# Delta-rule attention with an MLP: products with the state by head, in row and column tiles of 64

## The chip, the cores and the metric

The kernel runs on one core of a Trainium2 chip. The metric is the device time of one execution in microseconds; for the kernel before it is the median of nine executions. A profile is one execution taken by the hardware profiler. In it PE is the matmul side of TensorE and PEld its weight loads, DVE is VectorE, ACT is ScalarE, POOL is GpSimd and SP the engine that issues most DMAs.

## The reference

Four sequences (b), eight heads (h), 768 steps, head size 48. Each head has a state matrix of 48x48 that a delta rule updates step by step; its outputs, laid side by side to 384 columns, go through an MLP with a quick GELU.

```python
k_n = k / (np.linalg.norm(k, axis=-1, keepdims=True) + 1e-06)
state = np.zeros((B, H, D, D))
for t in range(S):
    y[:, :, t] = np.einsum('bhd,bhde->bhe', q[:, :, t], state)
    v_old = np.einsum('bhde,bhd->bhe', state, kt)          # kt, vt, bt: step t of k_n, v, beta
    state = state + bt * np.einsum('bhd,bhe->bhde', kt, vt - v_old)
x = y.transpose(0, 2, 1, 3).reshape(B * S, H * D)          # 3072 x 384
h = x @ w_in                                               # 384 x 2048
out = (h * (1.0 / (1.0 + np.exp(-1.702 * h)))) @ w_out     # 2048 x 384
```

## The kernel before

**Units.** The steps are cut into six chunks of 128. A unit is one chunk c of one sequence b, 24 units in all, c in the outer loop and b in the inner one. Within a chunk the recurrence is written as a triangular system: with G the products of keys by keys and keys by queries, and V the values, one solves for U, the corrected values times beta. The chunk has four blocks of 32 steps. The 32x32 diagonal blocks are inverted on VectorE for two sequences at a time (`invert`); the inverses go out to DRAM and come back as XB.

**One unit.** `prepare` transposes keys and queries to kqT (two heads to a partition half each: the head h lies on the partitions from h % 2 * 64, in the slot h // 2) and forms G in psG (L368). The class `Step` does the rest.

- `keys` (L501): V must lose the product of the keys with the state of the chunks before. S_bd keeps the state of two heads as a block-diagonal matrix of 128 rows by 2 x 48 columns, so four matmuls of the full array with 96 columns give all heads. They go to a bank psR that the unit keeps for its whole life.
- `above` (L512) adds to psR, block by block, the products with the U of the blocks above; `rest` (L520) takes 32 rows of psR from V on VectorE; `solve` (L524) multiplies by the inverse, in 32x32 tiles, and `solved` (L531) copies U on ScalarE.
- `queries` (L537): the transposed product of the state with the queries, per head, 48 output rows on the partition half of the head, into one bank psY; `outputs` adds U by G to the same places, then copies psY to xT, the input of the MLP.
- `state` (L556): four matmuls of the full array give keys by U for two heads each; VectorE adds the two diagonal blocks to S_bd (L564), in two instructions.

An xT tile has 128 partitions and three slots of 384/128. Six of the eight heads go to rows 0 to 47 and 64 to 111 of the three slots; the last two are copied to `last` (L576), and six DMAs bring their rows in pieces of 16 into the rows 48 to 63 and 112 to 127 of xT (L583). The rows of w_in are loaded in the order that fits (`x_rows`).

**The MLP.** `hidden` (L599) is xT by w_in into ph, followed by the GELU on ScalarE; `written` (L614) is its result by w_out into po. Both are generators, cut in small pieces. The weights come as float64 and are made float32 by VectorE and ScalarE (`from_double`); this lasts into the fifth slot or so.

**Order.** `slot(n)` interleaves the stages of three units that overlap: A is unit n-1, B_ is unit n, D_ is unit n+1. It has six groups, after each of which some matmuls of the MLP are taken from a queue (`take`), and pieces of the inversion, of the norms and of the weight conversion are put in. Group 0 is `above` and `rest` of block 2 of A; group 1 `solve` of block 2 of A beside `above` of block 1 of B_; group 2 `above` of block 3 of A, then `keys` and `rest(0)` of D_, then the last psG pair of `prepare`; group 3 three `solve`s in three tiles of the array and `queries` of A; group 4 `state` of A; group 5 `outputs` of A. The first two slots are pinned to this order. After that a planner orders each engine's instructions by its own costs, with the order of the program as priority, and gives out the PSUM banks: `ps_seq` has four, for psR, psU, psY and psS, `ps_big` two for psT and psG, `ps_moe` two.

Of the kernel before, what the change touches and what calls it, by code (L numbers as in the profile page):

```python
# [18 lines left out]
def kernel(  # L19
# [122 lines left out]
    S_bd = cpool.tile([128, B, NP, 2, D], F32, name="S_bd")  # L142
# [21 lines left out]
    def from_double(dst, raw, n, alone):  # L164
# [38 lines left out]
        (hh * DP + o, r, m, step)  # L203
        for hh in range(2)
        for o, r, m, step in (
            (0, hh * D, D, 2 * D), (D, (2 * KC + hh) * D, XR, XR),
        )
# [280 lines left out]
    class Step:  # L488


        def __init__(self, n, xT):
            self.c, self.b = units[n]
            self.xT = xT
            self.kn, self.kqT, self.G = ready.pop(n)
            self.V, self.XB = loaded.pop(n), inverse.pop(n)
            self.psR = bank("psR")
            self.U = wk.tile([128, H, D], F32, tag="U", name="U", bufs=3)

        def with_state(self, ps, i):
            for j in range(NP):  # L500
                pe.matmul(  # L501
                    ps[:, 2 * j : 2 * j + 2, :], lhsT=self.kqT[:, j, i, :],
                    rhs=S_bd[:, self.b, j], start=(j == 0), stop=True, skip_group_check=True,
                )

        def keys(self):
            if self.c > 0:
                self.with_state(self.psR, 0)

        def above(self, blk, h):  # L510
            r, a = slice(blk * BS, (blk + 1) * BS), slice(0, blk * BS)
            pe.matmul(  # L512
                self.psR[r, h, :], lhsT=self.G[a, h, 0, r], rhs=self.U[a, h, :],
                start=(self.c == 0 and h == 0), stop=True, skip_group_check=True,
            )

        def rest(self, blk):
            r = slice(blk * BS, (blk + 1) * BS)
            if self.c > 0 or blk > 0:
                vec.tensor_tensor(self.V[r], self.V[r], self.psR[r], op=ALU.subtract)  # L520
# [12 lines left out]
        def turned(self, lhsT, rhs, start):  # L533

            for h in range(H):
                j, p = h // 2, h % 2 * 64
                pe.matmul(  # L537
                    self.psY[p : p + D, j, :], lhsT=lhsT(h), rhs=rhs(h),
                    start=start and j == 0, stop=True, skip_group_check=True,
                )  # L540

        def queries(self):
            self.psY = bank("psY", (128, NP, 128))
            if self.c > 0:
                self.turned(
                    lambda h: S_bd[h % 2 * 64 : h % 2 * 64 + D, self.b, h // 2, h % 2, :],
# [276 lines left out]
```

## Time and profile before

| | |
|---|---|
| median of 9 executions | 858.25 us (854.8 to 860.56) |
| the profiled execution | 860.51 us, span 858.8 us |
| mean granted clock | 0.968 |
| PE busy | 807.4 us, 94% |
| PEld busy | 596.0 us, 69% |
| DVE busy | 495.2 us, 58% |
| ACT busy | 208.6 us, 24% |
| POOL busy | 107.9 us, 13% |
| share of the chain that ended last: PE | 80% |
| po L614, ph L599 | 28% each of the chain |
| psY L537, psR L512, psG L368, psU L524 | 5%, 4%, 4%, 4% of the chain |
| psR L501 (keys), psS L556 | 2% each of the chain |

Busy times are unions: two matmuls that overlap count once, so busy time divided by the count of a group is not the duration of one, and its mean duration has a tail that overlaps the next. The chain is followed back from the last instruction, at each step to what released it. In the timeline the start of one group to the start of the next is what a group takes where PE never idles.

### The profile page before, as it was taken

The numbers are of one execution on the slowest core, as the hardware profiler recorded it, in microseconds if no ns is written. First come the engines' busy times: TensorE is split into PE (matmuls) and PEld (weight loads), VectorE is DVE, ScalarE is ACT, GpSimd is POOL, SyncE is SP. The second block draws the span as 40 slices with busy tenths as digits, with TensorE's granted clock in tenths as the row PEclk, the third lists the DMA queues.
The fourth block names the chain that finished last, engine by engine and source line by source line (L and its number), as shares of the span: only waits on it lengthen the run. The fifth ranks groups of instructions, "written<-read, shape, count | busy, mean of one in ns | idle before, by whom it ended". The sixth has DMA issues, their size and how long they took to land.

```text
span 858.8 us, 15548 instructions
## 1 busy us (share of the span) xinstructions
PE 807.4 (94%) x6564; PEld 596.0 (69%) x6564; DVE 495.2 (58%) x1024; ACT 208.6 (24%) x407; POOL 107.9 (13%) x117
## 2 busy tenths in 40 slices
PE   8309999989999999999999999999999999999998
PEld 7207688557767767767767767767768768677684
DVE  5898789879992782772772872772862850110100
ACT  3202554233312312212213212212212112112020
POOL 2103232130021102101101110111100000000000
PEclk9759789999999999999999999999999999999999
DMA  9897553631323132132132132042032020000000
GB/s 146 180 151 150 145 141 86 150 90 46 70 69 68 31 76 64 27 84 62 20 85 63 20 86 61 19 87 52 11 79 50 2 57 2 10 15 1 22 2 18
DMA packets 160964, 55.75 MB, mean 65 GB/s; under 512 B 128672, under 2 KB 157568, under 8 KB 160896
## 3 DMA queue, kind: packets, MB, share of 16 engines
q1 hardware_dynamic: 154048, 46.02, 26.7%
q0 software_dynamic: 1856, 7.87, 2.9%
q10 hardware_dynamic: 4992, 0.89, 1.0%
q8 instruction: 51, 0.84, 0.4%
q14 instruction: 17, 0.14, 0.1%
HBM read 33.13 MB, written 20.45 MB: 62 GB/s over the span
## 4 chain that ended last, share of the span: by engine, by line
PE 80%; DVE 10%; DMA 7%; issue 2%; POOL 1%; ACT 1%; ACTq 0%; SPq 0%; DVEq 0%; POOLq 0%
PE po L614 28%; PE ph L599 28%; PE psY L537 5%; PE psR L512 4%; PE psG L368 4%; PE psU L524 4%; DMA w_out<-in_moe_w_out_dram 2%; DVE P L104 2%; PE psR L501 2%; PE psT L354 2%; PE psS L556 2%; DVE YB L104 1%; DMA w_out<-in_moe_w_in_dram 1%; DVE w_in L104 1%; DMA bI<-in_beta_dram 1%
## 5 line engine op out<-in xcount | busy, mean ns | idle before, releaser
L614 PE MATMUL po<-w_out,gT 128*128 128x384 f32 x768 | 267.8, 494 | 3.5 <-DVE w_out L192 3.5
L599 PE MATMUL ph<-xT,w_in 128*128 128x256 f32 (+1 forms) x1248 | 270.8, 371 | 0.3 <-DMA xT<-last 0.2
L599 PEld LDWEIGHTS ph<-xT,w_in 128*128 128x128 f32 x1248 | 220.4, 193 | 38.8 <-issue 11.9
L614 PEld LDWEIGHTS po<-w_out,gT 128*128 128x128 f32 x768 | 139.9, 190 | 94.9 <-issue 8.9
L604 ACT ACTIVATE gT<-ph 128x512 f32<-128x512 f32 (+1 forms) x104 | 58.6, 564 | 189.8 <-PE ph L599 189.8
L520 DVE TENSOR_TENSOR V<-V,psR 32x384 f32<-32x384 f32 x88 | 48.4, 550 | 90.6 <-PE psR L512 84.8
L531 ACT COPY U<-psU 32x384 f32<-32x384 f32 x89 | 41.8, 469 | 140.4 <-PE psU L524 88.8
L512 PEld LDWEIGHTS psR<-U,G 64*32 64x32 f32 (+2 forms) x1088 | 49.9, 107 | 21.9 <-issue 19.2
L512 PE MATMUL psR<-U,G 64*32 64x48 f32 (+2 forms) x1088 | 59.7, 205 | 1.5 <-ACT U L531 1.5
L392 POOL TENSOR_SCALAR_AFFINE_SELECT G<-G 128x1024 f32<-128x1024 f32 x24 | 28.0, 1168 | 240.7 <-DVE G L376 128.4
L152 PE MATMUL ps_warm<-ident 128*128 128x256 bf16 x152 | 22.8, 318 | 35.1 <-DVE ps_warm L104 32.8
L368 PE MATMUL psG<-kqT 48*128 48x256 f32 x352 | 54.7, 411 | 0.3 <-DVE G L376 0.3
L621 DVE COPY o<-po 128x384 f32<-128x384 f32 x24 | 13.3, 555 | 70.8 <-PE po L614 70.6
L524 PEld LDWEIGHTS psU<-V,XB 32*32 32x32 f32 x1424 | 34.3, 105 | 22.5 <-issue 10.4
L432 DVE TENSOR_TENSOR P<-NT,YB 64x2 f32<-64x2 f32 (+4 forms) x135 | 46.3, 343 | 4.3
L436 DVE TENSOR_REDUCE YB<-P 64x2 f32<-64x2 f32 (+4 forms) x135 | 43.3, 321 | 4.3
L152 PEld LDWEIGHTS <-ident 128*128 128x128 bf16 x152 | 17.0, 114 | 39.7 <-DVE ps_warm L104 33.2
L524 PE MATMUL psU<-V,XB 32*32 32x48 f32 x1424 | 41.3, 203 | 1.5 <-DVE V L520 1.4
L372 ACT ACTIVATE G<-psG 128x512 f32<-128x512 f32 x44 | 26.3, 597 | 65.3 <-PE psG L368 63.9
L576 DVE COPY last<-psY 48x128 f32<-48x128 f32 x20 | 5.9, 294 | 59.0 <-ACT xT L577 58.1
L368 PEld LDWEIGHTS psG<-kqT 48*128 48x128 f32 x352 | 33.3, 191 | 9.2 <-issue 2.6
L304 POOL TENSOR_TENSOR ksq<-KN 128x384 f32<-128x384 f32 x17 | 14.6, 857 | 177.3 <-DMA KN<-in_k_dram 177.3
(112 smaller groups left out, 784.5 us busy)
## 6 DMA issues: line engine op xcount, KB each, us to landing
Nd<-G SPq DMA_DIRECT2D x24, 512.0 KB, 3.3
w_out<-in_moe_w_out_dram POOLq DMA_DIRECT2D x14, 384.0 KB, 4.5
KN<-in_k_dram SPq DMA_DIRECT2D x24, 192.0 KB, 3.4
V<-in_v_dram SPq DMA_DIRECT2D x24, 192.0 KB, 3.3
out_dram<-o SPq DMA_DIRECT2D x24, 192.0 KB, 1.9
QP<-in_q_dram SPq DMA_DIRECT2D x20, 192.0 KB, 3.1
w_out<-in_moe_w_in_dram SPq DMA_DIRECT2D x6, 576.0 KB, 12.1
NT<-Nd SPq DMA_DIRECT2D x24, 128.0 KB, 2.5
```

Source lines behind the costliest of these rows:

```text
L152: pe.matmul(ps, lhsT=ones[:, 0:128], rhs=ones, start=True, stop=True)
L368: pe.matmul(ps[hh][:, i], lhsT=kqT[pr, g + i, 0, :], rhs=kqT[pr, g + i, :, :], start=True, stop=True,)
L432: tt(P, diag(Nf, i * BS, [[0, i], [1, i]]), diag(Yf, 0, [[BS, i], [1, i]]), op=ALU.mult,)
L436: red(diag(Yf, i, [[BS, i]]), P, axis=AX.X, op=ALU.add, negate=True)
L512: pe.matmul(self.psR[r, h, :], lhsT=self.G[a, h, 0, r], rhs=self.U[a, h, :], start=(self.c == 0 and h == 0), stop=True, skip_group_check=True,
L520: vec.tensor_tensor(self.V[r], self.V[r], self.psR[r], op=ALU.subtract)
L524: pe.matmul(psU[r, h, :], lhsT=self.XB[r, h, :], rhs=self.V[r, h, :], start=True, stop=True,)
L531: act.copy(self.U[r], psU[r])
L537: pe.matmul(self.psY[p : p + D, j, :], lhsT=lhsT(h), rhs=rhs(h), start=start and j == 0, stop=True, skip_group_check=True,)
L599: pe.matmul(ph[:, u], lhsT=w_in[:, j, f * 128 : (f + 1) * 128], rhs=xT[:, j, t], start=(j == 0), stop=(j == KC - 1),)
L604: act.activation(gT[f0 // FQ][:, f0 % FQ : f0 % FQ + 2, t], ph, ACT.Gelu_apprx_sigmoid)
L614: pe.matmul(po, lhsT=gT[f // FQ][:, f % FQ, i * C : (i + 1) * C], rhs=w_out[:, f, :], start=(f == 0), stop=(f == FC - 1),)
```

## The change

The state is kept as ST: head h on its 48 partitions, in the slot h // 2, without the zero blocks, and 16 further columns at the end of each sequence. `keys` has a matmul per head now, with the 48 rows of that head, in two row tiles of the array (0 and 64), each to a bank of its own (psK); their results are subtracted from all 128 rows of V at once, in one instruction for each bank. psR holds only the products of `above` and is taken anew for each block; `rest(0)` is gone. `turned` takes 64 weight columns per head instead of 48 (the last 16 belong to the next head, or to the padding of ST and of the fixed U buffers US), and puts the head h at the column tile h // 4, in the bank h % 2. `queries` goes through its heads in an order that visits all four tiles of 64x64. `state` has a matmul per head in two column tiles, and one addition over 128 partitions. psY is copied 128 partitions wide; the spilled rows are overwritten by the DMAs from `last`. The rows of w_in are permuted to suit.

```diff
-    S_bd = cpool.tile([128, B, NP, 2, D], F32, name="S_bd")
+    ST = cpool.tile([128, B, NP * D + XR], F32, name="ST")
+    US = [cpool.tile([128, H * D + XR], F32, name=f"US{i}") for i in range(3)]
...
     x_rows = [
-        (hh * DP + o, r, m, step)
-        for hh in range(2)
-        for o, r, m, step in (
-            (0, hh * D, D, 2 * D), (D, (2 * KC + hh) * D, XR, XR),
-        )
+        (ct * DP + o, (ct * NP + i) * D, m, step)
+        for ct in range(2)
+        for o, i, m, step in ((0, 0, D, D), (D, KC, XR, XR))
     ]
...
-            self.psR = bank("psR")
-            self.U = wk.tile([128, H, D], F32, tag="U", name="U", bufs=3)
-
-        def with_state(self, ps, i):
-            for j in range(NP):
+            self.US = US[n % len(US)]
+            self.U = self.US[:, 0 : H * D].rearrange("p (h d) -> p h d", h=H)
+
+        def rows(self, h):
+            return slice(h % 2 * 64, h % 2 * 64 + D)
+
+        def keys(self):
+            if self.c == 0:
+                return
+            psK = [bank("psK", (128, NP, D)) for _ in range(2)]
+            for h in range(H):
+                j = h // 2
                 pe.matmul(
-                    ps[:, 2 * j : 2 * j + 2, :], lhsT=self.kqT[:, j, i, :],
-                    rhs=S_bd[:, self.b, j], start=(j == 0), stop=True, skip_group_check=True,
+                    psK[h % 2][:, j, :], lhsT=self.kqT[self.rows(h), j, 0, :],
+                    rhs=ST[self.rows(h), self.b, j * D : (j + 1) * D], start=True, stop=True,
                 )
-        def keys(self):
-            if self.c > 0:
-                self.with_state(self.psR, 0)
-
+            for hh in range(2):
+                Vh = self.V[:, hh::2, :]
+                vec.tensor_tensor(Vh, Vh, psK[hh], op=ALU.subtract)
...
-        def turned(self, lhsT, rhs, start):
-            for h in range(H):
-                j, p = h // 2, h % 2 * 64
+        def turned(self, order, lhsT, rhs, start):
+            for h in order:
+                p, s = h // NP * DP, h % NP // 2
                 pe.matmul(
-                    self.psY[p : p + D, j, :], lhsT=lhsT(h), rhs=rhs(h),
-                    start=start and j == 0, stop=True, skip_group_check=True,
+                    self.psY[h % 2][p : p + DP, s, :], lhsT=lhsT(h), rhs=rhs(h),
+                    start=start and s == 0, stop=True, skip_group_check=True,
                 )
         def queries(self):
-            self.psY = bank("psY", (128, NP, 128))
+            self.psY = [bank("psY", (128, 2, 128)) for _ in range(2)]
             if self.c > 0:
                 self.turned(
-                    lambda h: S_bd[h % 2 * 64 : h % 2 * 64 + D, self.b, h // 2, h % 2, :],
-                    lambda h: self.kqT[h % 2 * 64 : h % 2 * 64 + D, h // 2, 1, :],
+                    (0, 5, 4, 1, 2, 7, 6, 3),
+                    lambda h: ST[self.rows(h), self.b, h // 2 * D : h // 2 * D + DP],
+                    lambda h: self.kqT[self.rows(h), h // 2, 1, :],
                     True,
                 )
         def state(self):
...
-            psS = bank("psS", (128, NP, 2, D))
-            for j in range(NP):
+            psS = bank("psS", (128, NP, D))
+            for h in range(H):
+                p = h % 2 * DP
                 pe.matmul(
-                    psS[:, j],
-                    lhsT=self.kn[:, 2 * j : 2 * j + 2, :].rearrange("p a d -> p (a d)"),
-                    rhs=self.U[:, 2 * j : 2 * j + 2, :], start=True, stop=True,
+                    psS[p : p + DP, h // 2, :], lhsT=self.kn[:, h, :], rhs=self.U[:, h, :],
+                    start=True, stop=True,
                 )
-            for hh in range(2):
-                pr = slice(hh * 64, hh * 64 + 64)
-                St = S_bd[pr, self.b, :, hh, :]
-                vec.tensor_tensor(St, psS[pr, :, hh, :], St, op=ALU.add)
+            St = ST[:, self.b, 0 : NP * D].rearrange("p (j d) -> p j d", j=NP)
+            vec.tensor_tensor(St, psS, St, op=ALU.add)
         def outputs(self):
-            self.turned(lambda h: self.U[:, h, :], lambda h: self.G[:, h, 1, :], self.c == 0)
+            self.turned(
+                (0, 4, 1, 5, 2, 6, 3, 7),
+                lambda h: self.US[:, h * D : h * D + DP], lambda h: self.G[:, h, 1, :],
+                self.c == 0,
+            )
...
-            for hh, copy in ((0, act.copy), (1, other)):
-                p = slice(hh * 64, hh * 64 + D)
-                copy(last[p, t], self.psY[p, KC, :])
-                copy(self.xT[p, :, t], self.psY[p, 0:KC, :])
+            other(last[:, t], self.psY[1][:, 1, :])
+            act.copy(self.xT[:, 0::2, t], self.psY[0])
+            other(self.xT[:, 1, t], self.psY[1][:, 0, :])
...
                 if A:
+                    psR = bank("psR")
                     for h in range(H):
-                        A.above(2, h)
-                    A.rest(2)
+                        A.above(2, h, psR)
+                    A.rest(2, psR)
...
                     D_.keys()
-                    D_.rest(0)
...
-    nc.gpsimd.memset(S_bd, 0.0)
+    nc.gpsimd.memset(ST, 0.0)
+    for U in US:
+        nc.gpsimd.memset(U[:, H * D :], 0.0)
```

Groups 1 and 2 take psR for `above` of blocks 1 and 3 in the same way as group 0 does for block 2.

## The prediction

> **What bounds the kernel now.** I read first the page's forty slices, for where TensorE (PE) has holes.
>
> ```profile
> PE   8309999989999999999999999999999999999998
> DVE  5898789879992782772772872772862850110100
> PEclk9759789999999999999999999999999999999999
> ```
>
> From the ninth slice on PE is full at full clock; before that VectorE (DVE) is as full as PE. The table of stretches (span, PE busy, weight loads, DVE, ScalarE, GpSimd, clock, DMA) puts numbers on it:
>
> ```profile
> 160.00:200.00 40.00, 36.37 (x341) 22.64 (x340) 31.62 (x78) 15.04 (x32) 10.27 (x11) 1.00 0.48 110
> 200.00:300.00 100.00, 100.00 (x823) 75.83 (x822) 73.74 (x152) 26.89 (x52) 14.54 (x12) 1.00 0.26 56
> 500.00:600.00 100.00, 100.00 (x866) 73.72 (x867) 52.84 (x99) 23.60 (x46) 13.84 (x13) 1.00 0.30 65
> 700.00:800.00 100.00, 100.00 (x796) 72.97 (x795) 11.15 (x22) 17.13 (x35) 0.00 (x0) 1.00 0.04 10
> ```
>
> So there are two regimes. Up to about 190 us, DVE and the DMA of w_out set the pace (the last wait of PE, 2.36 us for a converted w_out, ends at 189.55). From there to 855 us PE never idles, and one microsecond of PE work is one microsecond of time. The timeline of one slot (start, length, line, tile, array rows*columns, shape, count) shows what is in that work:
>
> ```profile
> 499.92 0.88 PE L524 MATMUL psU<-V,XB 32*32 32x48 f32 x48
> 500.73 1.08 PE L537 MATMUL psY<-kqT,S_bd 48*48 48x128 f32 x16
> 501.74 4.14 PE L614 MATMUL po<-w_out,gT 128*128 128x384 f32 x12
> 505.71 1.03 PE L556 MATMUL psS<-U,KN 128*128 128x96 f32 x8
> 506.57 2.77 PE L614 MATMUL po<-w_out,gT 128*128 128x384 f32 x8
> 509.28 1.08 PE L537 MATMUL psY<-G,U 128*48 128x128 f32 x16
> 510.29 2.85 PE L614 MATMUL po<-w_out,gT 128*128 128x384 f32 x8
> ...
> 525.50 1.13 PE L501 MATMUL psR<-S_bd,kqT 128*128 128x96 f32 x8
> 526.57 1.14 PE L368 MATMUL psG<-kqT 48*128 48x256 f32 x8
> 527.63 4.15 PE L599 MATMUL ph<-xT,w_in 128*128 128x256 f32 x18
> ```
>
> Every matmul of the code stands there twice (two fp32 passes). The lengths include a tail that overlaps the next row, so I use start-to-start. Products with the state: queries 1.01 us, state 0.86, keys 1.07; outputs, not with the state but in the same function as the queries, 1.01.
>
> **The rates behind them.** In the tail of the kernel 96 ph passes of 256 columns run from 813.77 to 834.50: 216 ns each, 0.84 ns a column. So a pass over 128 columns streams 108 ns, over 48 columns 41 ns. psS streams 96 columns (81 ns) yet takes 0.86/8 = 108 ns: it is bound by its load of 128 weight columns, again 0.84 ns a column; 64 columns make 54 ns, 48 make 40. Now the tiled groups: psU has 48 passes of about 42 ns in 0.81 us, which fits only if its three tiles run together (16 x 42 = 0.67, rest 0.14). Queries have 16 passes of 108 on two tiles: 8 x 108 = 0.865, rest 0.145. psG, two row tiles: 4 x 216 = 0.864, rest 0.20. The rest is what a change of tile shape costs at entry: about 0.09 of draining plus the first load, bare (27, 40 and 107 ns for these three). Do loads of different tiles overlap too? The start of a psG group says so:
>
> ```profile
> 519.56 0.30 PEld L368 LDWEIGHTS psG<-kqT 48*128 48x128 f32 x4
> ```
>
> One load's row lasts 0.187, so the fourth starts 0.11 after the first: two pairs, 107 ns apart. One at a time they would start 0.32 apart.
>
> **What the Trainium skill says.** "TensorEngine Tiling (Array Packing)", Key Properties: tiles load and multiply in parallel, and changing the tiling mode drains TensorE; the trace agrees (three tiles of psU at once; 0.09 us of drain). The same page, Gotcha 1: different row tiles must use different PSUM banks; psG does, with two, and the new keys and queries put each row tile in its own bank. "TensorE: Matmul & The Clock Gate", LDWEIGHTS: the load's time goes with the weight columns, not the rows; agreed (128 columns 107 ns). The same page, Measured speedup vs the span model: nine tiles[...] in row and column together ran 6.3 times faster; no row here shows four tiles of 64x64 at once. The two halves of that are shown: psG has two row tiles over the same columns, outputs two column tiles over the same rows, each at full rate.
>
> **The change part by part (PE, after 190 us).**
>
> Queries, 20 units, all after 215 us. Two tiles become four, in an order that visits all four: 16 passes in 4 rounds of 108 instead of 8, so -0.432; the first load has 64 columns instead of 48, +0.013. 20 x -0.419 = -8.4 us. The four-way overlap is the term the trace does not show. Its bounds: nothing gained (two at a time: +0.3 us in all) and the full -8.4; I take the full value, since each pair of tiles is seen overlapping.
>
> Keys. 8 passes with 128-column loads become 16 in two row tiles, each of them 8 loads of 107: if the loads overlap, the length stays. But the group now has psG's tile shape, and psG follows it directly: its entry (0.09 drain, 0.107 bare load) goes, less about 0.02 for a shorter cover of the last pass: -0.18. That adjacency holds for 15 units after 190 us: -2.7. Three units (682, 712, 740 us) are followed by MoE matmuls of the full array, into which keys used to run without a break: +0.13 each, +0.4. Sum -2.3. If the loads were one at a time, keys would grow by 8 x 0.107 = 0.86 each, +15 us; the psG row above excludes that.
>
> State, 16 units after 190. Before: 0.86 and about 0.03 in the next load, no change of shape against its neighbours. After: entry 0.09 + 0.054; 8 rounds on two column tiles, each bound by a load of 54 plus some 4: 0.46; exit 0.09 + 0.107. Together 0.80, so -0.09 each, -1.5. Serial loads would make it 1.27, +6 us; the outputs' two column tiles, which keep 108 ns a pair with two 40-ns loads inside, do not exclude that strictly, so it belongs to the range.
>
> Outputs: the same rounds, first load 64 columns: about 21 x 0.013 = +0.3.
>
> Sum on PE: -8.4 - 2.3 - 1.5 + 0.3 = -11.9 us.
>
> **DVE, ScalarE, DMA.** The durations:
>
> ```profile
> L520 DVE TENSOR_TENSOR V<-V,psR 32x384 f32<-32x384 f32 x88 | 48.4, 550 | 90.6 <-PE psR L512 84.8 <-PE psR L501 4.5
> L564 DVE TENSOR_TENSOR S_bd<-psS,S_bd 64x192 f32<-64x192 f32 x38 | 13.4, 354 | 17.9 <-PE psS L556 17.5
> L577 DVE COPY xT<-psY 48x384 f32<-48x384 f32 x20 | 11.1, 553 | 0.0
> ```
>
> Keys' subtraction: one of 550 becomes two over 192 elements, 2 x 354: +0.16. State: 2 x 354 become one: -0.35. Copies of psY: DVE 294 + 553 become 2 x 294 (-0.26); ScalarE 258 + 470 become one of 256 elements, 381 by the gT row of that size (-0.35). DVE loses 0.45 us a unit and ScalarE 0.35: nothing after 190 us, where PE hides both. Both engines could read psY one after the other only (one bank); now side by side. The two subtractions stand ahead of psG's copy on DVE and of the solve of block 0: in the slot shown rest(0) ends at 527.2 and psU starts at 531.71, with ph between; the least such slack after 240 us is about 2.2 us, against 0.16 more. The six DMAs xT<-last now wait for the copies of xT too (they write over spilled rows): at most 0.4 us later, on SP ahead of loads that are used slots later, and at the end the hidden layer starts 4.9 us after the last outputs. Weight rows are permuted, in equal pieces: 0. Memsets on GpSimd get smaller: 0.
>
> Before 190 us, four or five units have no keys or queries; DVE saves 0.35 in each state update, about -1.4, against +0.3 for two units' keys, in a stretch where it is nearly full. But psR, one bank held per unit, becomes a bank per block, two for keys, two for psY: ten allocations a slot from four banks instead of five, each freed by a DVE or ScalarE instruction, and DVE lags here. I take -0.3 for both together, with -2 and +15 (below) as ends.
>
> Total -12.2. The profiled execution: span 858.8 in 860.51 us, so 846.6 in 848.3. Its time is 2.3 above the median of 858.25; from the median, 846.
>
> **Rivals.** (1) Four tiles do not run together, only pairs: -11.9 loses 8.7, so about 854.5. For it: no such row before. Against: the pairs. (2) The planner, whose costs and free banks change, takes keys away from psG, splits groups or places them between MoE matmuls, each at 0.3 us of entry and exit: half the gain gone, 852. The page shows it: near 230 us the outputs are split into 10 and 6 passes. (3) Slower: banks held while DVE lags. Around 140 to 220 us a subtraction of V started up to 10 us after its psR matmuls (keys at 209.4, the later of the two subtractions behind them at 220.2, after eight operations of the inversion). Then psK's two banks stay taken, psR of the other unit holds a third, and queries, which now want two banks, wait at the head of PE's queue with all MoE work behind. A lag of 10 against a cover of 4 us of MoE costs 6 a time; the case decides from two such stalls on (12 us) and gives about 864 at three. Against it: after 240 us the lag is at most 3.5 us, less than the cover, and the planner can put MoE work first. (4) Nothing measurable: gains and some stalls cancel, 858. That the products aren't changed as said is excluded by the diff.
>
> **How the numbers follow.** Main case 843 to 850: 0.64. Pairs only 0.12; planner 0.08; both lie in 850 to 855.5. Within 0.3% (2.6 us, about what a measurement of this kernel tells from no change) 0.06; slower 0.10. The range 842 to 855.5 leaves out the last two and a little. Faster 0.84.
>
> **What would show it.** Queries 1.01 to about 0.58 us start-to-start, with psY in four forms of one shape; keys about 1.05 and psG behind it 0.87 instead of 1.06; psS 16 passes in about 0.6, with 0.2 in the matmul behind; PE still 100% in each stretch after 200 us; DVE about 9 us less in all. Wrong if queries stay at 1.0, if keys takes 1.9, if psS takes 1.1, or if PE shows waits for DVE or ScalarE before psK, psY or psR.

## The result, and the profile after

The changed kernel takes 852.6 us (median of 11 executions, 850.17 to 855.57) against 858.51 for the kernel before beside it: a ratio of 0.993, 95% interval 0.9909 to 0.9951. It is faster by 6 us, about half of the forecast 12.2. The profiled execution took 851.28 us, its span is 849.2. The page's slices of the changed kernel, in the order shown of before:

```profile
PE   8308999899999999999999999999999999999998
DVE  5798879978992592682682772872762840110100
```

TensorE's row is full from the ninth slice on (before it was from the tenth, not the ninth as the prediction says); two slices ahead of it have a tenth less than before. The table of stretches of the changed kernel (span, PE, weight loads, DVE, ScalarE, GpSimd, clock, DMA) is finer. Between 200 and 300 us, PE is idle for 1.5 us, where it was never idle before. In the stretch ahead of it the granted clock is 0.96, where it was 1.00; this comes back in the early part, below.

```profile
160.00:200.00 40.00, 37.82 (x348) 23.32 (x347) 31.81 (x79) 13.86 (x29) 10.33 (x11) 0.96 0.44 110
200.00:300.00 100.00, 98.51 (x899) 72.83 (x898) 73.22 (x151) 27.03 (x50) 15.03 (x12) 1.00 0.26 58
```

The timeline of one slot of the changed kernel (start, length, line, tile, array rows*columns, shape, passes) has the groups that the prediction priced:

```profile
241.01 1.09 PE L513 MATMUL psK<-ST,kqT 48*128 48x48 f32 x16
241.93 1.10 PE L369 MATMUL psG<-kqT 48*128 48x256 f32 x8
242.96 4.14 PE L630 MATMUL po<-w_out,gT 128*128 128x384 f32 x12
247.03 0.88 PE L534 MATMUL psU<-V,XB 32*32 32x48 f32 x48
247.84 0.67 PE L550 MATMUL psY<-kqT,ST 48*64 48x128 f32 x16
248.43 2.85 PE L630 MATMUL po<-w_out,gT 128*128 128x384 f32 x8
251.21 0.67 PE L572 MATMUL psS<-US,KN 128*64 128x48 f32 x16
251.81 2.85 PE L630 MATMUL po<-w_out,gT 128*128 128x384 f32 x8
254.59 1.09 PE L550 MATMUL psY<-G,US 128*64 128x128 f32 x16
255.62 1.56 PE L630 MATMUL po<-w_out,gT 128*128 128x384 f32 x4
```

Start to start, queries take 0.59 us (were 1.01), state 0.60 (0.86), keys with the psG behind them 1.95 (2.13), outputs 1.03 (1.01). The mechanism of the forecast is there at its size, but for psG behind the keys. DVE's subtraction of the keys in the changed kernel (count, busy, mean ns, idle before):

```profile
L519 DVE TENSOR_TENSOR V<-V,psK 128x192 f32<-128x192 f32 x40 | 12.6, 351 | 4.9 <-PE psK L513 4.6
```

The addition to the state takes 353 ns and a copy of psY 280. The prediction had taken 354, 354 and 294 from rows of the kernel before. DVE is busy 482.8 us in all, 12.4 less.

**Where the time went.** The keys of the third unit of chunk 1 start at 209.4 us in the kernel before and at 208.9 in the changed one, and from there to the end every kernel below has the same MLP work left (1020 ph and 704 po passes in the records). That rest of the span fell from 649.4 to 640.3 us, by 9.1. The forecast for it was 11.7: all of the -11.9 but about 0.2. So some 2.6 us are missing after that point, and, since the median fell by 6 and not by 9, about 3 are missing ahead of it, where the two profiled executions alone show nothing (the early stretch of one kernel scatters by 2 us or so from execution to execution).

The 2.6 us can be seen. This is PE's only wait after 205 us in the changed kernel, from the table of waits (us in all, times, longest):

```profile
PE psY L550 <- DVE V L519: 1.5, 1, 1.5
```

Its place, in PE's timeline (the releaser of the idle time in brackets):

```profile
215.16 0.65 PE L550 MATMUL psY<-kqT,ST 48*64 48x128 f32 x8
215.74 3.29 PE L615 MATMUL ph<-xT,w_in 128*128 128x256 f32 x14
220.52 0.65 PE L550 MATMUL psY<-kqT,ST 48*64 48x128 f32 x8 [1.49 <-DVE V L519]
```

And on DVE, in the same stretch:

```profile
217.99 2.09 DVE L417 TENSOR_REDUCE YB<-P 64x64 f32<-64x768 f32 x2
220.12 0.35 DVE L519 TENSOR_TENSOR V<-V,psK 128x192 f32<-128x192 f32 x1
220.50 1.22 DVE L467 TENSOR_TENSOR YS<-YB,bI 64x1024 f32<-64x1024 f32 x1
221.75 0.35 DVE L519 TENSOR_TENSOR V<-V,psK 128x192 f32<-128x192 f32 x1
```

The keys of 208.9 filled two banks. DVE empties the first at 220.1, behind the inversion of the next sequences. With psU and the first half of psY the four banks are taken, so the queries of the unit ahead are cut into two groups of eight passes, and the second one waits with all of PE's queue behind it. By pairs of neighbouring records, the wait and the second group cost about 2.2 us. The rest is, by the timelines, a loss of about 0.6 us at 450 us: the six DMAs xT<-last take longer on SP than in the slot of the kernel before (3.88 us for the six),

```profile
445.23 5.31 SPq L599 DMA_DIRECT2D xT<-last  x6
```

and the hidden layer that reads xT is late by that much. (In other slots these six took 3.7 to 4.4 us in the changed kernel and 3.7 to 4.9 us before, so one slot says little.)

### The profile page after: what moved, and what is told of

It reads as the page before. It is cut to its first block, busy times and chain, and to the rows that moved or that the text cites. A ratio compares the mean times of both kernels' runs of the same rounds, so it can differ in the third digit from the quotient of the medians.

```text
span 849.2 us, 16185 instructions
## 1 busy us (share of the span) xinstructions
PE 794.1 (94%) x6884; PEld 578.8 (68%) x6884; DVE 482.8 (57%) x1024; ACT 200.8 (24%) x383; POOL 106.1 (12%) x120
## 4 chain that ended last, share of the span: by engine, by line
PE 79%; DVE 12%; DMA 5%; issue 1%; POOL 1%; ACT 1%; ACTq 0%; DVEq 0%; POOLq 0%
PE po L630 29%; PE ph L615 27%; PE psG L369 4%; PE psR L523 4%; PE psY L550 4%; PE psU L534 4%; PE psK L513 2%; DVE P L104 2%; PE psT L355 2%; DMA w_out<-in_moe_w_out_dram 2%; DVE YB L104 1%; DMA w_out<-in_moe_w_in_dram 1%; DVE w_in L104 1%; PE psS L572 1%; PE ps_warm L104 1%
## 5 line engine op out<-in xcount | busy, mean ns | idle before, releaser
L615 PEld LDWEIGHTS ph<-xT,w_in 128*128 128x128 f32 x1248 | 221.3, 194 | 41.5 <-issue 11.1
L530 DVE TENSOR_TENSOR V<-V,psR 32x384 f32<-32x384 f32 x68 | 37.6, 553 | 90.6 <-PE psR L523 89.5
L541 ACT COPY US<-psU 32x384 f32<-32x384 f32 x89 | 41.8, 469 | 139.9 <-PE psU L534 82.3
L523 PEld LDWEIGHTS psR<-US,G 64*32 64x32 f32 (+2 forms) x1088 | 50.0, 107 | 19.4 <-issue 19.0
L523 PE MATMUL psR<-US,G 64*32 64x48 f32 (+2 forms) x1088 | 59.8, 205 | 0.0
L409 DVE TENSOR_TENSOR NT<-NT,bI 64x1024 f32<-64x1024 f32 x9 | 11.9, 1328 | 42.8 <-DMA NT<-Nd 42.8
L591 DVE COPY last<-psY 128x128 f32<-128x128 f32 x20 | 5.7, 287 | 53.1 <-PE psY L550 53.1
```

The source lines that it names most:

```text
L523: pe.matmul(psR[r, h, :], lhsT=self.G[a, h, 0, r], rhs=self.U[a, h, :], start=True, stop=True,)
L530: vec.tensor_tensor(self.V[r], self.V[r], psR[r], op=ALU.subtract)
L541: act.copy(self.U[r], psU[r])
L615: pe.matmul(ph[:, u], lhsT=w_in[:, j, f * 128 : (f + 1) * 128], rhs=xT[:, j, t], start=(j == 0), stop=(j == KC - 1),)
```

## The experiments

Ratios are to the kernel before on the same chip, with 95% intervals. "The rest of the span" is the stretch from the keys of the third unit of chunk 1 on, from one profiled execution each. Waits are PE's.

**Both kernels once more.** No edit.

> The kernel before once more, for a second trace of it and for the spread. Theory A (the missing 6 us lie before about 209 us, where the kernel waits for weights and VectorE): from the keys of the third unit of chunk 1 (209.45 us in the first trace) to the end this trace takes 649.3 us again, to 0.5 us, and all spread is ahead of that point. Theory B (they lie in the part where TensorE is full): that stretch itself varies by several us between executions.

> The changed kernel once more. From the keys of the third unit of chunk 1 to the end the first trace took 640.3 us, 9.1 less than before, of the 11.7 that my sum has for that stretch. Theory A: 640.3 again to 0.5 us, and the start of that stretch later than 208.96, near 210.5, since the median is 1.3 us above the profiled execution; so about 3 us are lost ahead of it. Theory B: the start stays at 209 and the stretch takes 642 or more.

> The changed kernel itself, for a comparison on the same chip with the three others: ratio to the kernel before 0.9925 to 0.993, about 852.

Before again: 1.0017 (0.9989 to 1.0045), rest of the span 649.4 as before. The changed kernel: 0.9924 (0.9906 to 0.9943) and 0.9947 (0.993 to 0.9964, above its forecast), rest of the span 640.1 and 641.6, from 210.4 and 211.0 us on. That is theory A. So the rest of the span repeats within 0.3 us, but for the last (1.3): in that execution the clock granted to TensorE was at half for 3.4 us from 223.5, where PE was full, which accounts for up to 1.7 us. The ratios of one kernel differ by up to 0.2%.

**The order of the heads.** Queries visit two tiles twice before the other two:

```diff
-                    (0, 5, 4, 1, 2, 7, 6, 3),
+                    (0, 5, 2, 7, 4, 1, 6, 3),
```

> The changed kernel with one edit: queries go through the heads in an order in which each tile of 64x64 gets its two heads one after the other, so that two tiles run at once for most of the group. My sum: a group of queries goes back from 0.58 to about 0.9 to 1.0 us and the kernel is 6.5 to 8.5 us slower than the changed one (859 to 861). Rival (the order of heads is not what gives the 0.58, the array reorders by itself, or the gain is lost behind something else): within 1.5 us of the changed kernel.

0.9959 (0.9931 to 0.9987), rest of the span 640.9. In PE's timeline of that kernel the group still takes 0.61 us to the next start:

```profile
250.49 0.68 PE L550 MATMUL psY<-kqT,ST 48*64 48x128 f32 x16
251.10 1.24 PE L630 MATMUL po<-w_out,gT 128*128 128x384 f32 x3
```

The theory that the order is what brings four tiles together falls. First to last pass is 412 ns against 398. The program as built has the edited order in 19 of its 20 groups, so the planner did not put the passes back; the records of the execution do not name the head, so what lets them overlap all the same stays open. The kernel is 2.8 us slower than the changed one beside it, more than the 1.5 of the rival; 0.8 of it lies in the rest of the span, with one more wait (0.4 us for XB), and the others ahead of it.

**One part alone.** Each is added to the kernel before. State:

```diff
-            for j in range(NP):
-                pe.matmul(
-                    psS[:, j],
-                    lhsT=self.kn[:, 2 * j : 2 * j + 2, :].rearrange("p a d -> p (a d)"),
-                    rhs=self.U[:, 2 * j : 2 * j + 2, :], start=True, stop=True,
+            for h in range(H):
+                p = h % 2 * DP
+                pe.matmul(
+                    psS[p : p + DP, h // 2, :], lhsT=self.kn[:, h, :], rhs=self.U[:, h, :],
+                    start=True, stop=True,
```

> The kernel before with the new state products alone (a matmul per head in two column tiles, one bank, still two additions). My sum: a group goes from 0.86 to about 0.6 with 0.2 more in the matmul behind it; 1.5 us less in the same stretch, 647.8, and the kernel at 857. Theory D: nothing lost ahead of it. Rival: the start is later by 1 us or more, since the two changes of tile shape per unit also fall into the part that waits for weights.

0.9984 (0.9966 to 1.0002), -1.4 us where the sum said -1.5, but the interval just includes nothing. Its one trace does not show the gain in the rest of the span: 649.1 us where 647.8 was expected, with the keys' group cut there and a wait of 0.7 us for V. Keys, with psR taken anew for each block as in the change:

```diff
-            self.psR = bank("psR")
...
+            psK = [bank("psK", (128, NP, D)) for _ in range(2)]
+            for h in range(H):
+                j = h // 2
+                pe.matmul(
+                    psK[h % 2][:, j, :], lhsT=self.kqT[self.rows(h), j, 0, :],
+                    rhs=S_bd[self.rows(h), self.b, j, h % 2, :], start=True, stop=True,
+                )
```

> The kernel before with the new keys alone (a matmul per head in two row tiles, two banks psK, subtracted from all of V; psR taken anew for each block); queries, state and outputs as before. My sum: 2.3 us less in the stretch from the keys of the third unit of chunk 1 to the end (649.3 to 647.0). Theory D (the 3 us lost ahead of that stretch come from the banks: psR by block and psK): they are lost here too, and the kernel stays at 858 to 859.5. Rival (they come from another part): 856.3.

1.0007 (0.9992 to 1.0022): no gain, as theory D had it. The rest of the span is 1.0 us shorter, of 2.3 in the sum, with a wait of 1.1 us for XB in it; what it gains there is lost ahead. Queries and outputs with their copies, with psR still held by the unit (`spill` gives the 64 weight columns of a head out of the block-diagonal state):

```diff
-            self.psY = bank("psY", (128, NP, 128))
+            self.psY = [bank("psY", (128, 2, 128)) for _ in range(2)]
...
+                    (0, 5, 4, 1, 2, 7, 6, 3),
+                    lambda h: self.spill(h),
```

> The kernel before with the part of the queries and outputs alone: four tiles of 64x64, psY in two banks, outputs and copies 128 partitions wide; keys and state as before (full array, psR kept by the unit). By the sum: 20 x -0.419 for the queries and 0.3 for the outputs, so -8.1 us after the keys of the third unit of chunk 1 (649.3 to about 641.2), those keys at 207 to 208.5 us as before, in all about 850, ratio 0.9905. Rival 'psY's banks': if the second bank of psY while VectorE lags makes the early loss, the start is 3 us later: 853, ratio 0.994.

1.0054 (1.0039 to 1.007): slower than before by 4.6 us, where both theories had a gain. The rest of the span grew by 5.3 us. PE's timeline of that kernel in a late slot:

```profile
497.82 0.88 PE L538 MATMUL psU<-V,XB 32*32 32x48 f32 x48
498.63 0.65 PE L554 MATMUL psY<-kqT,S_bd 48*64 48x128 f32 x8
499.21 1.56 PE L636 MATMUL po<-w_out,gT 128*128 128x384 f32 x4
500.70 0.65 PE L554 MATMUL psY<-kqT,S_bd 48*64 48x128 f32 x8
```

and ScalarE's, the copies of U that set psU free:

```profile
498.78 1.43 ACT L545 COPY US<-psU 32x384 f32<-32x384 f32 x3 [4.33 <-PE psU L538]
```

The queries stand in two groups of eight in 18 of the 20 slots. Two units hold a psR, psU takes the third bank and the first half of psY the fourth, so the second half, as the rows stand, goes where psU has been copied. A half is one row tile and two column tiles: eight passes take 0.58 us, as long as all sixteen do when four tiles run together. Two halves take 1.16 us instead of 1.01, and eighteen more groups are entered and left between MLP passes. PE shows no wait for it. The kernel two paragraphs below has these queries with a psR by block, at 0.9909, and its groups are whole. It differs from this one in the state's products and the keys' bank too, so that the release of psR between blocks makes the gain possible is likely, but no run changes it alone.

**The subtractions of the keys ahead of the inversion.**

```diff
-            for hh in range(2):
-                Vh = self.V[:, hh::2, :]
-                vec.tensor_tensor(Vh, Vh, psK[hh], op=ALU.subtract)
+            with tc.high_priority():
+                for hh in range(2):
+                    Vh = self.V[:, hh::2, :]
+                    vec.tensor_tensor(Vh, Vh, psK[hh], op=ALU.subtract)
```

> The changed kernel with the two subtractions of the keys' products put ahead of other ready work on VectorE by the planner. Theory C (banks of psK are held while VectorE does the inversion; one such wait of 1.49 us ahead of queries at 220.5, and that group and others split around it): the wait for V goes, the queries of the sixth unit stay one group, and 1.5 to 2.5 us are won against the changed kernel. Rival (that wait only takes the place of another wait, or the new order of VectorE delays the inversion): no gain, within 1 us, or a loss.

0.994 (0.9918 to 0.9962), no gain on the changed kernel. The queries are whole again and the wait for psY is gone, but PE now waits for psU, 1.9 us in all after 205 us instead of 1.5:

```profile
PE psU L535 <- DVE V L531: 1.6, 2, 1.1
PE psU L535 <- DMA XB<-Yd: 0.3, 1, 0.3
```

So the wait has moved, as the rival had it.

**The keys back to the full array, all else as changed**: one bank, one subtraction over 384 columns; the state is block-diagonal again, with two additions.

```diff
-            psK = [bank("psK", (128, NP, D)) for _ in range(2)]
-            for h in range(H):
-                j = h // 2
+            psK = bank("psK")
+            for j in range(NP):
                 pe.matmul(
-                    psK[h % 2][:, j, :], lhsT=self.kqT[self.rows(h), j, 0, :],
-                    rhs=ST[self.rows(h), self.b, j * D : (j + 1) * D], start=True, stop=True,
+                    psK[:, 2 * j : 2 * j + 2, :], lhsT=self.kqT[:, j, 0, :],
+                    rhs=S_bd[:, self.b, j], start=True, stop=True,
                 )
```

> The changed kernel with the keys' products back in the full array with the block-diagonal state: four matmuls, one bank psK, one subtraction of 128x384; psR still by block; two additions to the state. My sum: 2.3 us more in the stretch (642.4). Theory D in the form that psK's second bank does the harm: the 1.49 us wait and the split of queries go, and the start comes forward by 2 to 3 us, so 849.5 to 851. Rival: 854.5, the start as in the changed kernel.

0.9909 (0.988 to 0.9939), 850.4 us, where the theory had it. The rest of the span is 2.2 us longer than in the changed kernel, as the sum has it, and yet the time is lower by some 2: the keys of the third unit start at 206.0. What the row-tiled keys gain is lost ahead of that stretch, and more. The wait for psY and the cut of the queries are gone, but PE waits after 205 us all the same, 2.5 us for psU.

**psR held by the unit in chunk 0 only.**

```diff
+            self.psR = bank("psR") if self.c == 0 else None
...
-                    psR = bank("psR")
+                    psR = A.psR if A.c == 0 else bank("psR")
```

> The changed kernel with one edit: in chunk 0 (no keys there) a unit keeps one bank psR for its life, as before the change. The stretch to the end stays at 640.1. Theory D in the form that psR by block is what loses the time at the start: the start comes forward by 2 to 3 us and the kernel is at 849 to 850. Rival: 852, as the changed kernel, to 1 us.

0.9939 (0.992 to 0.9958), as the rival had it: psR by block, in chunk 0, does not cause the early loss. (Its rest of the span is 642.1, not 640.1; half clock for 3.4 us from 223.0 accounts for up to 1.7 of that.)

**Banks or subtractions.** The kernel with the keys back in the full array, with two subtractions of 192 columns, from one bank and then from two (with two matmuls to each):

```diff
-            vec.tensor_tensor(self.V, self.V, psK, op=ALU.subtract)
+            for p in range(2):
+                Vp = self.V[:, p * NP : (p + 1) * NP, :]
+                vec.tensor_tensor(Vp, Vp, psK[:, p * NP : (p + 1) * NP, :], op=ALU.subtract)
```

```diff
-            psK = bank("psK")
+            psK = [bank("psK", (128, NP, D)) for _ in range(2)]
```

> The changed kernel with the keys as four matmuls of the full array into one bank, as in the run with the keys put back, but V is lessened by two subtractions over 128x192 instead of one over 128x384. Theory 'second bank': what the changed kernel loses ahead of the keys of the third unit of chunk 1 comes from the second bank that the keys hold while VectorE lags; then nothing is lost here: those keys start at about 205 to 206.5 us, from there to the end 642 to 643 us, about 850 us in all. Rival 'second subtraction': VectorE's queue is what is late, and a second instruction in it costs as much: 208.5 to 210, about 853.

> As the run before it in this list, but the four matmuls of the keys go to two banks, two to each, with one subtraction for each bank. Theory 'second bank': the start of the changed kernel comes back without row tiles: the keys of the third unit of chunk 1 start at about 209 to 210.5 us, the time is 853 to 855 us, since the 2.3 us that row tiles save after it are missing. Rival 'second subtraction': the same as with one bank and two subtractions. Rival 'row tiles': the loss comes with the row tiles and the half subtractions that read every other head; then 205 to 206.5, about 850 us here too.

One bank: 0.9912 (0.9883 to 0.994), rest of the span 640.8 (642 to 643 was expected), the keys of the third unit at 205.9. The queries are whole; the waits after 205 us are

```profile
PE psU L538 <- DVE P L434: 1.2, 1, 1.2
PE psU L538 <- DVE V L534: 0.4, 1, 0.4
```

Two banks: 0.9923 (0.9896 to 0.995), rest 643.1, and PE waits again as in the changed kernel:

```profile
PE psY L555 <- DVE V L524: 1.5, 1, 1.5
```

with the queries in two groups of eight at 214.0 and 219.8 us. So the second bank makes that wait, row tiles or not, and the split with it. But without it PE waits as long for the same lagging DVE, a little later: it moves the wait more than it makes one. Of the 2.4 us between the two rests, half clock for 3.4 us from 221.6 in the second execution accounts for up to 1.7. For the early part the run speaks against the second bank: those keys started at 207.6 us, between the 209 to 210.5 of the theory and the 205 to 206.5 of its rivals, and the ratio makes 851.6 us, not 853 to 855. The second subtraction costs nothing that shows.

**The mixed kernel.** The keys of chunk 1 as full array from one bank, those of later chunks in row tiles from two; in the second kernel the later subtractions also go first.

```diff
+            if self.c == 1:
+                psK = bank("psK")
+                for j in range(NP):
+                    pe.matmul(
+                        psK[:, 2 * j : 2 * j + 2, :], lhsT=self.kqT[:, j, 0, :],
+                        rhs=S_bd[:, self.b, j], start=True, stop=True,
+                    )
+                vec.tensor_tensor(self.V, self.V, psK, op=ALU.subtract)
+                return
```

> The state block-diagonal with two additions; the keys of chunk 1, where VectorE lags, as four matmuls of the full array into one bank with one subtraction; from chunk 2 on in row tiles and two banks as in the changed kernel; all else as in the changed kernel. If start and steady part add up: keys of the third unit of chunk 1 at about 205 to 206.5 us, from there 640.5 to 641.5 us (the full-array form costs 2.3 over 15 units, two of them here), in all 847.5 to 848.8 us. If the 2.3 us were not the keys' form but a wait that comes back elsewhere: 850 or more.

> As the mixed kernel, and the two subtractions of the keys of the later chunks go ahead of the waiting instructions of VectorE. If banks held by late subtractions still cost something after chunk 1, up to 1 us faster than the mixed kernel, 847 to 848; if it only exchanges one wait for another, as in the run where the subtractions of all chunks went first, the same within 0.5 us.

> The mixed kernel with the later subtractions first, once more: ratio 0.988 to 0.9895, some 3 us below the changed kernel beside it. If its lead was chance: within 1 us of it.

The mixed kernel: 847.78 us, 0.9893 (0.987 to 0.9917). With the subtractions first: 846.75 us, 0.9888 (0.9863 to 0.9914), and once more, beside the changed kernel at 853.63: 848.25, 0.9895 (0.9863 to 0.9927). The two forms cannot be told apart. The second beats the changed kernel on the same chip by 4 to 5 us of 858; the first, on another chip, is lower by 3 to 4. In the mixed kernel the queries after the same keys stay whole (PE's timeline),

```profile
214.79 0.67 PE L564 MATMUL psY<-kqT,S_bd 48*64 48x128 f32 x16
215.38 6.96 PE L631 MATMUL ph<-xT,w_in 128*128 128x256 f32 x31
```

though DVE empties the keys' bank as late as ever (DVE's timeline):

```profile
219.50 0.56 DVE L522 TENSOR_TENSOR V<-V,psK 128x384 f32<-128x384 f32 x1
```

and the rest of the span is 638.3 us, 11.1 shorter than before, with one wait of 0.9 us for psU. The forecast, less the 0.4 that its two units of full-array keys there cost, is 11.3. With the subtractions first the rest is only 9.0 shorter in both runs, with waits of 2.5 and 2.6 us for psU in it, so the same time comes there from an earlier start (203.5 and 205.0 us). The mixed kernel's forecast was met in sum and by luck: its keys of the third unit started at 208.4 us, not at 205 to 206.5, and the rest was shorter than the 640.5 to 641.5 that were expected.

**The mirror**: row tiles and two banks in chunk 1 only.

```diff
-            if self.c == 1:
+            if self.c > 1:
```

> The mirror of the mixed kernel: the keys of chunk 1 in row tiles and two banks, those of the later chunks as four matmuls of the full array into one bank; the state block-diagonal, all else as in the changed kernel. Theory 'form in chunk 1': what the changed kernel loses early comes with the row-tiled keys of its four units of chunk 1, whatever the mechanism; then this kernel has that loss and pays the 2.3 us of the full-array form as well: 853.5 to 855, ratio about 0.995 to 0.996. Rival 'scatter': the early stretch only differs from program to program by chance, not by this form: 850 to 851.5, ratio 0.991 to 0.9925.

0.9947 (0.9925 to 0.9968), 853.33 us, as the theory "form in chunk 1" had it; the mixed kernel with the subtractions first, on the same chip, was at 0.9895. The wait is back: 1.1 us for psY, with the queries in two groups of eight. Of the 4.5 us between them, 3 lie in the rest of the span (643.5 against 640.4), and by the sum about 2 of these are the price of full-array keys in the later chunks. The closer partner is the kernel with all keys in the full array (0.9909), which differs from the mirror in chunk 1 alone: it is 3 us faster, though on another chip and with intervals that just overlap.

**The early part, from all runs.** The ratio times 858.25 us gives each kernel's change; less the change of the rest of the span, it leaves what happened ahead of it:

| keys of chunk 1 | kernel: change, rest of the span, ahead (us) |
|---|---|
| row tiles, two banks | changed: -6.0, -9.1, +3.1; again: -6.5, -9.3, +2.8; again: -4.5, -7.8, +3.2; other order of heads: -3.5, -8.5, +5.0; subtractions first: -5.1, -9.6, +4.4; psR by unit in chunk 0: -5.2, -7.3, +2.1; keys alone: +0.6, -1.0, +1.6; mirror: -4.5, -5.9, +1.4 |
| full array | before again: +1.5, 0.0, +1.5; state alone: -1.4, -0.3, -1.0; queries alone: +4.6, +5.3, -0.7; keys put back: -7.8, -6.9, -0.9; one bank, two subtractions: -7.6, -8.6, +1.1; two banks: -6.6, -6.3, -0.4; mixed: -9.2, -11.1, +1.9; mixed, first: -9.6, -9.0, -0.6; again: -9.0, -9.0, 0.0 |

Eight runs with row tiles in chunk 1 lose 3.0 us on average, nine without lose 0.1. A single entry is uncertain by some 2 us, so this rests on the two groups and not on one run.

**The granted clock.** The traces show where most of this goes. Between 125 and 205 us the clock granted to TensorE (the third number from the end) is lower with row-tiled keys in chunk 1. The rows are of the kernel before, of the changed kernel once more, of the kernel with the keys put back, and of a part of the changed kernel's stretch:

```profile
125.00:205.00 80.00, 74.87 (x704) 54.68 (x703) 69.59 (x151) 30.44 (x66) 18.50 (x20) 1.00 0.43 100
125.00:205.00 80.00, 73.16 (x680) 52.28 (x680) 66.61 (x149) 27.35 (x60) 18.40 (x20) 0.94 0.43 99
125.00:205.00 80.00, 74.63 (x685) 53.35 (x684) 69.86 (x150) 28.54 (x63) 18.23 (x20) 1.00 0.43 99
174.80:181.60 6.80, 6.80 (x19) 3.87 (x18) 5.99 (x14) 1.70 (x3) 3.41 (x3) 0.50 0.32 100
```

The clock falls to half there, for pieces of 3.4 us or twice that, and PE's passes take nearly twice as long in them. (Ahead of 125 us every trace has 44 to 58 us of it.) In the changed kernel once more, around the keys of the second unit of chunk 1:

```profile
174.30 1.17 PE L630 MATMUL po<-w_out,gT 128*128 128x384 f32 x2 [0.74 <-DVE w_out L195]
...
178.25 3.87 PE L630 MATMUL po<-w_out,gT 128*128 128x384 f32 x6
182.05 0.28 PE L534 MATMUL psU<-V,XB 32*32 32x48 f32 x4
```

The same passes with full-array keys from one bank and two subtractions:

```profile
171.50 0.91 PE L636 MATMUL po<-w_out,gT 128*128 128x384 f32 x2 [0.65 <-DVE w_out L196]
...
173.60 2.20 PE L636 MATMUL po<-w_out,gT 128*128 128x384 f32 x6
175.73 0.27 PE L538 MATMUL psU<-V,XB 32*32 32x48 f32 x4
```

Both kernels cut the keys' group at a wait for w_out; but six passes take 3.80 us to the next start in the one and 2.13 in the other. Between 125 us and the keys of the third unit all eight traces with row tiles have 3.4 to 10.2 us at half clock. Of the other ten only the mixed kernel's has any (6.8 us), and its entry above, +1.9, is the largest of its row. In the mean of the executions whose clock is on record, it is 0.9645 with row tiles in chunk 1 (92 executions) and 0.9685 without (198); 0.004 of 850 us is 3.4 us, an estimate of the most that this can cost. In the 18 traces, the keys of the third unit start the later, the more time at half clock lies ahead of them (203.3 us with 44 us of it, 210.4 and 211.0 with 65; correlation 0.86). So the early loss goes with lost clock, at about its size. No run changed the clock by itself, and why row-tiled keys there lower it is open.

## Why the prediction was wrong, and what in it was right

**Queries, -8.4.** Right. The four-way overlap, the term that the kernel before did not show, came in full: 0.42 us a unit, first to last pass 398 ns instead of 808. Rival 1, pairs only, did not happen when the group is whole. But the price held for whole groups alone, and the step never said what keeps them whole. The queries alone show it: where psR stays with the unit, nearly each group falls into two halves of two tiles, and the same matmuls cost 5 us instead of saving 8.

**Keys, -2.3.** Right in sum: 0.18 less for keys and psG together. The split between the two was not: the saving stands on the keys (1.07 to 0.92), since psG behind them keeps 1.03 where 0.87 was forecast.

**State, -1.5, and outputs, +0.3.** State went from 0.86 to 0.60 with the rest in the groups around it; by pairs of records it saves 1.5 over 15 units. Its own run gave -1.4, which is not clear of nothing. Outputs +0.02 a unit.

**The sum after 190 us, -11.9.** The changed kernel got 9.1 of 11.7, the mixed kernel 11.1 of 11.3. The prices held to about 1 us, and waits were missing: with PE's waits in that stretch added back, the changed kernel comes to 11.3 (its wait and cut group are 2.2), the mixed kernel with the subtractions first to 11.5 of 11.3, the kernel with the keys put back to 9.4 of 9.4, and the keys alone to 2.1 of 2.3. The mixed kernel (12.0) and one bank with two subtractions (10.2 of 9.4) go past their sums.

**"xT<-last ... at most 0.4 us later".** Too low in one slot: about 0.6, where the six DMAs took 5.31 us and not only started later.

**The step that failed: "I take -0.3 for both together" before 190 us.** The stretch ahead of the keys of the third unit of chunk 1 lost about 3 us where a small gain was taken. The term set DVE's savings against banks, and took TensorE's clock there as it was in the kernel before, without giving a reason. Neither psR by block nor the second bank of the keys was found to cause the loss; what the traces show in its place is the clock at half for 6.8 to 10.2 us in the three traces of the changed kernel, between 125 us and those keys, and for none in the two traces before. That the loss comes with the row-tiled keys of chunk 1 rests on two groups of runs; how these bring the clock down stays open.

**A second step failed: "PE still 100% in each stretch after 200 us".** Of the 11.7 us after 209 us, 2.2 went to one wait of 1.49 us and the cut group beside it. This is the effect that the prediction had named as rival 3, "banks held while DVE lags", and left out of the sum. Its place was right (keys at 208.9, subtractions at 220.1 and 221.8, queries at the head of PE's queue), and so was its mechanism: a lag of 11 us on DVE, two banks instead of one. Its price was not: "6 a time" set a lag of 10 against 4 us of MLP work, while the planner cut the queries, put fourteen more ph passes between the halves and left 1.49 us of wait, once. The other part of it, cut groups, was rival 2, priced at 0.3 us each for the tile change; here a cut group costs its parallel half as well, 0.58 us for half the passes. Both were cases beside the main one, all or nothing; they happened at a third of their size, in the main case. And the lag is more than its bank: where the second bank or the order of the subtractions was taken away, PE waited 0.9 to 2.6 us for psU instead. The last sign on the prediction's list, a wait for DVE before psY, is the one that showed.

**DVE about 9 us less**: 12.4 less, which as forecast brought nothing after 240 us.

"TensorEngine Tiling (Array Packing)", Gotcha 1: PSUM Pressure, of the Trainium skill says that row tiling raises the pressure on PSUM, since row tiles need banks of their own. The prediction counted the banks but put nothing for them into its sum after 190 us. The runs show sizes: 2.2 us where one pair of keys' banks was freed late, and for the queries alone 13 us between the forecast and the measurement. The same section says that different row tiles cannot access one bank at the same time. The kernel before does not agree: its queries went from two row tiles into one bank psY, each to its own half of the partitions, and 16 passes of 108 ns took 808 ns from first to last start, so two ran at once.

## What to carry to other kernels

Price a faster group together with what it holds: when a product is spread over more banks, count the banks taken at the moment it is issued, and look for the latest instruction that frees one of them, because a group cut at a bank loses its parallel tiles and not only a tile change. After taking such a wait away, look at the sum of the waits: here it mostly came back at the next product that the lagging engine feeds. A form that pays where one engine is the bound can cost where another lags, so try it from the point on where the wait is gone: here full-array keys in the first chunk with state and row-tiled ones later gave about 9 us instead of 6. Where a loss has no wait to show for it, compare the granted clock stretch by stretch, before and after. And add up a partial wait as a term of the main case rather than as a rival with a small chance.

## What the hardware showed unexpectedly

Four 64x64 tiles with float32 ran at the full rate of each: 16 passes of 128 columns in 398 ns from first to last start, against 385 ns for 8 passes on two column tiles of one row tile (the queries alone). The order in which the heads are written hardly matters for it, 412 against 398 ns. With row-tiled keys in chunk 1 the clock granted to TensorE fell to half for 3.4 us or more between 125 us and the keys of the third unit in every one of eight traces, and six passes of po took 3.80 us instead of 2.13. And six small DMAs that depend on copies from two engines took between 3.7 and 5.3 us of SP's queue in the changed kernel, depending on the slot.
